# Modulation vectors as columns that are spread under a matrix of ones, eleven spectrum buffers, and a new written-out order

## The chip, the cores and the metric

The kernel runs on one core of one Trainium2 chip. The metric is the device time of one execution in microseconds (us), lower is better; several executions are given as a median. A core has five engines with queues of their own: PE (TensorE: matmuls, with PEld for its weight loads), DVE (VectorE), ACT (ScalarE), POOL (GpSimd) and SP (SyncE, which here issues nearly all DMAs). Each engine takes its own instructions in the order in which they were written, and waits for others by semaphores. Matmul results land in PSUM; everything else lives in SBUF.

## The reference, cut to what matters

```python
x = A_q                                                  # 2048 x 640
sa, ca, ga, sb, cb, gb = split(silu(c) @ w_mod, 6)       # w_mod is 640 x 3840
h = layernorm(x) * (1 + ca) + sa
x = x + ga * A(h, k, v, ...)   # A: 4-tap conv of k, times v; a long convolution
                               # along the 2048 rows by FFT; y + kv * ssm_D; times h
h = layernorm(x) * (1 + cb) + sb
x = x + gb * B(h, ...)         # B: z = gelu(h @ w_in), halves z1 and z2;
                               # z2 = layernorm(z2); g = w_sp @ z2 + b_sp; (z1 * g) @ w_out
```

Everything is bfloat16 with 2048 rows, 640 channels and 1728 columns of `w_in` (two halves of 864).

## The kernel before, in words

**Layout.** `xt` holds the 2048 x 640 input as 16 row tiles of 128 partitions. `gh` holds, of the same shape, first the normalised x, then (by `gh_mod`, L648) that times `(1 + ca) * ga` plus `sa * ga`, so that the gate `ga` is already inside; for that, rows `gca1_bf` and `gsa_bf` (128 x 640, the same vector in every partition) are needed. `gb_bf` is the row of `gb`; it multiplies `w_o` in the last part. `cb` and `sb` are used as columns (channel on the partition).

**The loop over spectra.** Channels are taken in five units of 128 (`u` = 0 to 4). For every unit the filter (`XK`) and the signal (`XU`) go through a first transform stage (`s1`, copied by `s1c`), then eight steps `st` of a second one: `fwdK` on PE is copied by ACT into a `KH` tile (`khc`), `fwdU` on PE stays in PSUM (`pu`), DVE multiplies both (`prod`, L454), for six of eight steps two `csum` halves add up (L468, on POOL or DVE), `inv` on PE transforms back into `pz`, and `zc` (ACT or DVE) copies that into `Z`. For units 0 to 3 one DMA transpose (`zt`, L677) turns `Z` into `ZT`, of which there is one buffer; then PE does four `y` steps (`y u_0` to `y u_24`) and DVE multiplies them into `gh` (`ym`, L670). `res` (L690) adds `gh` into `xt`; `ln2` (L696) takes statistics. Unit 4 is turned on PE instead (`zfl`, copies `zk`, `yl`, `yml`).

**The signal.** k and v are loaded by DMA transposes (`ldk`, tag `big`, two buffers), convolved by PE (`taps`), multiplied by v on DVE (`tv`), written to a scratch in DRAM (`kvw`) and read back as `XU`.

**After the loop.** For each of four groups of four row tiles: `ag2`, `rstd2` (POOL), `nmr2`, `zx` (normalise, on DVE, ACT or POOL), turned on PE for group 0 (`hfl`, with `hmod` on DVE and ACT) and by a DMA (`turn`, with `hmod2`) for the others; then 16 `zz` matmul groups per row-tile group (5 matmuls of 432 columns each, alternating PSUM tags `pu` and `pz`, two buffers each), their gelus on ACT, and for the z2 half `stz`, `agz`, `rstdz`, `nmrz`, `zn`. Then comes the part that is not planned: `mix`, `project` (L969, L989).

**What sets the order.** `Plan.op` (L94) numbers every step as the code is built and records what it reads and writes. `Plan.run` (L112) then issues them in the order of the string `ORDER` (L40): each entry is an engine letter (P, A, D, G for POOL, S for SP) and a step's number. So `ORDER` fixes both the engine of a step and the order in each engine's queue. `FILLS` (L34) gives the lengths of dummy matmul groups (`fill`, L941) that write an `s1` PSUM tile. `SLOTS` (L36) gives the buffers per tag: KH=9, wm=1, T=3, sm=2, big=2, ZT=1.

**The modulation vectors.** `mod(j)` (L607) is called for j = 2, 1, 0, 3, 4, 5 (ga, ca, sa, sb, cb, gb). Each loads 640 x 640 weights `wm` (800 KB, one buffer). For j = 3 and 4 it makes columns: 25 matmuls with one moving column (`modc`), then a copy of 128x5. For the others it makes rows: per half of 320 columns five matmuls with `sc_rep` (silu(c) repeated 128 times, written by `scr` at L782) as weights (`modr`), so that every partition gets the row; then `gac` (ACT) for ga, `gcac` (DVE) for `(1 + ca) * ga`, `gsac` (DVE) for `sa * ga`, `gbc` (ACT) for gb. `gelut` (L784) is a one-element gelu that has the table for gelu loaded; nothing depends on it.

Of the kernel before, what the change touches and what calls it, by code (L numbers as in the profile page):

```python
# [10 lines left out]
ALU = mybir.AluOpType  # L11
# [4 lines left out]
P = 128  # L16
# [17 lines left out]
FILLS = (4, 6, 2, 2, 4, 3, )  # L34
MODE = ('susussus', 'susussus', 'susussus', 'susussus', 'susussus')
SLOTS = dict(Tf=2, W=2, X=3, X1=4, KH=9, T=3, Z=3, ZT=1, wm=1, big=2, dg=2, st1=2, s1=1, sm=2, pu=2, pz=2)  # L36
# [4 lines left out]
D0 D13 D100 G101 S88 A1 P1032 P7 A4 A10 G5 A23 D15 D102 D109 D103 D110 A112 D115 A111 S2 D6 P1033 P8 A11 D14 A16 D116  # L41
A117 A118 D104 A105 S19 P1034 P26 A106 D90 D121 S82 D86 D17 D122 D18 G119 G113 P1035 P145 A146 P148 D149 S21 S83 D87
P24 A124 A147 D27 D127 S20 A150 P227 A228 A114 P151 A123 A152 P154 A156 P28 D25 S22 A153 D29 D155 P233 A234 G125 A126
P30 S523 D31 D527 P139 D140 G120 S34 P161 A162 P163 S32 G107 P133 P229 G48 A164 S33 P169 A170 D134 D36 S3 P167 A168
A230 G108 P136 D137 P171 A172 P165 A166 P142 A143 G135 D528 P41 A128 D529 D530 D138 P157 A158 P159 A160 S35 G141 P231
A232 D42 S84 S85 P37 D38 P173 P176 A174 A175 D177 P43 D44 A178 P182 D183 P9 A12 G130 P179 A184 P39 D181 D40 A180 P185
D186 S524 A531 A532 P195 D196 P191 D192 S46 S47 P55 D56 A533 P247 A248 G187 G188 P189 S45 P211 D212 G197 G144 G198 P51
D52 A534 P201 D202 D535 P49 D50 G213 P205 G214 A190 S526 A542 P53 D206 P203 A204 G72 S89 P217 D218 G131 A543 P193 P221
D222 P251 A252 D194 P215 A216 A544 G536 D537 P235 P253 P199 D254 D54 A236 P241 A242 G60 S565 P566 G553 P257 A258 S525
D538 D539 S91 G207 G208 P237 P568 A238 P239 A240 P255 A256 G223 P245 D93 A246 P249 A250 S57 G549 G224 D554 G555 P225  # L50
A226 D200 P301 P259 D260 P291 D292 G556 P209 A302 P219 G261 G262 D540 S570 P303 A569 P269 A567 G550 G551 G552 D270
G271 P275 A304 A220 P573 D574 P307 A210 P571 D276 D572 G651 A308 P285 D286 D541 A545 P263 P293 S58 A294 P305 A306 P65
D614 P243 A264 P265 G707 D266 A244 D546 S92 P325 S59 D66 D672 G272 D593 A326 P63 D64 P315 A316 P327 D649 P273 G287
A328 P321 A322 D591 P267 A268 G288 P329 A330 S575 G547 D548 S70 P295 D296 D297 P578 D579 A274 P576 G561 D577 D562 D594
P313 A557 A314 P309 P331 A332 P61 D652 S94 D96 G298 D563 D564 G655 A310 P67 D62 P311 P375 D68 A312 P349 D350 P333 D334
P289 G597 D670 P73 A376 A558 A559 A560 P343 D344 P77 G598 P377 P317 A318 D129 A290 P277 A278 G335 D595 D596 A378 D653
G336 P323 A324 P299 D592 P337 A300 P319 A320 A338 G345 S71 D78 S599 G346 D74 D616 P379 A380 P369 G713 P600 G612 S69
P351 A352 P279 P347 D370 D601 P381 A382 P602 D280 D603 P365 P79 D366 D80 A348 G654 P604 P383 A384 S95 P399 A400 D605
P387 A388 P359 G281 G282 P283 A284 G371 G372 P401 A402 D360 P606 D607 G613 P353 D354 S97 P385 A386 D99 S580 D618 P403
A404 P75 P397 A398 P395 A396 D619 D671 P405 A406 P373 A374 P339 G361 G362 P363 A364 D615 P449 A450 G608 D76 P413 P367  # L60
A368 G355 D340 D414 P407 D408 P341 A342 G617 P453 G709 S620 P621 D622 G674 P393 D650 A454 P389 A394 A390 S81 G356 P623
D624 P451 A452 P439 D440 P357 A358 P625 D626 P391 A392 P455 P427 G409 G410 P627 P417 G609 P581 G673 G656 D428 G429
D430 A456 S98 P411 A412 D418 P471 A472 P473 D628 A474 D634 P431 P457 G419 G420 P443 P479 A458 D444 A480 D629 D632 P467
A468 P421 A432 P423 D424 G445 P475 A476 P433 D434 A582 S657 G639 A422 P415 G676 P461 A462 D631 P477 A478 D630 D638
P463 A464 P658 D659 A416 P465 A466 P441 A442 G446 P660 D635 P481 G435 P447 A448 P497 G710 D661 P662 G436 P437 A438
P425 A426 D482 D663 P664 D498 S583 P517 D518 G677 G483 G484 P485 A486 P507 D508 P499 P459 A460 P469 P501 A470 D665
G675 G519 G520 P521 A522 G509 G510 A500 A132 G708 P487 P584 D502 P513 D488 P511 A512 P491 P489 G503 A490 D514 P515
G504 D492 S678 G668 P505 P679 A516 A506 G493 D494 P495 A585 D633 D680 P681 D682 A496 P719 A720 D636 S586 P683 D684
P715 P721 A722 D716 P685 D686 D687 P717 A718 P587 A588 P723 P726 P725 G711 P724 G666 D688 D689 G714 D727 D728 D730
D729 D759 P735 P749 P589 A590 D758 D731 D732 G692 D690 G760 D761 D691 A762 G763 P1036 P1037 P764 D736 D733 P765 D771  # L70
D766 D767 D768 D734 D772 P742 G667 D693 D750 G773 D774 G775 D737 D740 D739 G610 D741 D738 D694 A769 S756 A770 P787
D637 P784 D696 A788 A776 S757 D695 D836 P818 G669 P791 A785 A792 P777 D835 D837 P778 D834 A782 A819 D779 D643 D780
D781 P816 A817 G838 D839 D840 D841 A783 P794 A795 P814 P820 A842 A821 D843 S844 G848 D697 D699 G845 A815 D702 D751
D753 D701 D712 D743 D700 D698 D744 D748 D903 P798 A799 P812 A813 P826 A827 D747 P805 A806 P808 P801 A809 P822 D703
D752 D642 D849 D754 A846 A847 D704 A802 P824 A825 P886 A823 D640 A887 P850 A851 D706 P853 D611 G644 A854 D641 P857
D745 A858 P884 D900 P874 D902 A885 D746 D901 G904 D905 A875 D906 D755 D909 D907 D800 P890 A891 P880 A881 P882 P892
G908 S910 A893 A883 D876 D705 P888 A889 G912 A911 P860 P871 D810 A872 D803 D646 D807 D967 P878 A861 A913 P864 D647
A865 P867 A879 A868 D915 D914 P958 D648 D969 P923 P916 A924 A917 P946 D786 A959 P944 D645 A947 D966 D968 G970 D971
D972 G973 D796 P937 D804 A938 D975 D789 D790 A945 P933 A934 P926 D793 D797 P930 A931 G974 S976 A981 D859 D869 D866
D870 A927 D811 G828 P954 A955 D918 P952 A953 P948 G978 D932 D935 D936 A979 P940 A941 P919 D939 A949 D829 A830 D873  # L80
D877 D942 D943 D928 G980 G977 P1020 A920 A1021 P982 A983 D925 D929 D921 A833 D852 D862 D863 P996 D855 D856 G894 D895
P1024 A1025 A997 D998 D922 P989 A990 D831 P992 D899 A993 P1006 A1007 P1003 D1008 P985 A1004 D991 A986 P1014 A1015 G960
D961 P956 A957 P999 P950 A1000 A832 D896 A951 P1010 A1011 D1005 D994 P1016 A1017 D898 D987 D984 D1001 D988 D1002 D995
P1022 D1009 G1026 D1027 A964 D1029 A1031 A965 P1012 D962 D1028 D897 P1018 A1019 A1023 A1013 D1030 D963
# [39 lines left out]
def kernel(  # L124
# [79 lines left out]
    with ExitStack() as actx:  # L204
        consta = actx.enter_context(tc.tile_pool(name="consta", bufs=1))
        gh = consta.tile([P, NT, D], BF16)
        ga = consta.tile([P, D], F32)
# [7 lines left out]
        sc_rep = consta.tile([P, ND, P], BF16)  # L215
# [53 lines left out]
        nc.gpsimd.memset(mhalf[:], -0.5)  # L269

# [336 lines left out]
        def mod(j):  # L607
# [6 lines left out]
            if j in (3, 4):  # L614
                ps = "mod%d" % j

                def cols(e):
                    p_ = new(ps, "sm", [P, 512], F32)
                    for i in range(ND):
                        for kt in range(ND):  # L620
                            mm(p_[:, i:i + 1], tl[wm][:, kt, i * P:(i + 1) * P], sc_bf[:, kt:kt + 1], kt == 0, kt == ND - 1)
                op("P", "modc", cols, r=[wm, "sc"], w=[ps], new=[(ps, "sm")])
                if j == 3:
                    op("A", "sbc", lambda e: e.copy(sb_col[:], tl[ps][:, 0:ND]), r=[ps], w=["sb"])
                else:
                    op("A", "cbc", lambda e: e.add(cb1_col[:], tl[ps][:, 0:ND], 1.0), r=[ps], w=["cb"])
                return
            for h in range(NH):
                ps, hs = "mod%d_%d" % (j, h), slice(h * HS, (h + 1) * HS)
                p_ = lambda ps=ps: tl[ps][:, 0:HS]  # L630

                def rows(e, ps=ps, hs=hs, p_=p_):
                    new(ps, "sm", [P, 512], F32)
                    for kt in range(ND):
                        mm(p_(), sc_rep[:, kt, :], tl[wm][:, kt, hs], kt == 0, kt == ND - 1)
                op("P", "modr", rows, r=[wm, "sc"], w=[ps], new=[(ps, "sm")])
                if j == 2:
                    op("A", "gac", lambda e, hs=hs, p_=p_: e.copy(ga[:, hs], p_()), r=[ps], w=[("ga", h)])
                elif j == 1:
                    op("D", "gcac", lambda e, hs=hs, p_=p_: e.scalar_tensor_tensor(  # L640
                        gca1_bf[:, hs], p_(), 1.0, ga[:, hs], op0=ALU.add, op1=ALU.mult), r=[ps, ("ga", h)], w=[("gca", h)])
                elif j == 0:
# [407 lines left out]
```

## Time and profile before

| what | us |
|---|---|
| median of four runs (318.89 to 321.42) | 319.88 |
| the profiled execution | 321.42 |
| its span | 319.6 |
| PE busy in the span | 307.7 |
| DVE busy | 205.5 |
| ACT busy | 153.2 |
| POOL busy | 113.2 |

The span is the time from the first to the last instruction of the profiled execution; 1.8 us lie around it. In the page's slices each digit is the busy share of a fortieth of the span in tenths. A line of the stretches gives start and end, length, then the busy time and number of instructions of PE, PEld, DVE, ACT and POOL, the clock granted to PE (1.00 is full), the share of the DMA engines' time and GB/s. A line of the order of time gives the start, the duration (of several alike, from the first start to the last end), the engine, the line of the code, the operation, output and inputs, shape, count, and in brackets how long the engine sat idle before it and what ended that. Matmuls overlap, so for PE the distance from one start to the next is what a step costs, not the duration shown.

### The profile page before, as it was taken

To read this page: it belongs to the slowest core of one execution; us is meant where nothing else is said; L and a number is where in the kernel's file an instruction comes from. 1 tells how busy PE (TensorE), PEld (TensorE's weight loads), DVE (VectorE), ACT (ScalarE), POOL (GpSimd) and SP (SyncE) were. 2 spreads that over 40 slices of the span, in tenths; PEclk is the share of its full clock that TensorE was granted. 3 is DMA by queue.
4 is the path that set the end of the run, shared out by engine and by line. 5 is a ranking of instruction groups with operands and counts; after the bars stand their busy time and mean duration, and the time that the engine had idled before them with its cause. 6 is when DMAs were issued, how large, how long until landed. Compare 5 with 4: busy or idle time off the path is not lost.

```text
span 319.6 us, 6393 instructions
## 1 busy us (share of the span) xinstructions
PE 307.7 (96%) x2570; PEld 204.3 (64%) x2577; DVE 205.5 (64%) x436; ACT 153.2 (48%) x273; POOL 113.2 (35%) x146
## 2 busy tenths in 40 slices
PE   7988899989999999999999999999999999999996
PEld 2755688758799988655555555555555555555554
DVE  7898998979999998898884872522222222333333
ACT  6987799978888867477667772000000000000001
POOL 2532877848987997544234310000000000000000
PEclk9999999999999999999999999999999999999999
DMA  8999999996988479022419960675556555522221
GB/s 167 205 229 227 239 297 246 216 188 161 237 201 159 128 144 368 4 42 41 84 33 161 184 174 2 131 165 106 134 115 117 115 115 117 115 51 49 49 51 62
DMA packets 127025, 45.00 MB, mean 141 GB/s; under 512 B 116143, under 2 KB 126228, under 8 KB 126996
## 3 DMA queue, kind: packets, MB, share of 16 engines
q1 hardware_dynamic: 126842, 44.55, 64.8%
q8 instruction: 20, 0.33, 0.4%
q14 instruction: 9, 0.07, 0.1%
q10 hardware_dynamic: 154, 0.05, 0.1%
HBM read 16.11 MB, written 5.24 MB: 67 GB/s over the span
## 4 chain that ended last, share of the span: by engine, by line
PE 60%; DMA 2%; DVE 1%; ACT 0%; issue 0%; SPq 0%
PE ps L974 29%; PE pz L237 10%; PE pu L237 10%; PE po L995 9%; DMA big<-in_B_w_in_dram 2%; PE sm L237 1%; DVE Tf L454 1%; PE s L237 1%; DVE T L454 0%; ACT X L240 0%; PE s L850 0%; DVE ot L997 0%; PE sm L850 0%; PE pt L986 0%; SPq L612 0%
## 5 line engine op out<-in xcount | busy, mean ns | idle before, releaser
L974 PE MATMUL ps<-X,wT 128*128 128x432 bf16 x512 | 95.7, 346 | 0.0
L974 PEld LDWEIGHTS <-wT 128*128 128x128 bf16 x512 | 50.1, 98 | 42.2
L987 ACT COPY uT<-pt 128x896 bf16<-128x896 bf16 x1 | 0.9, 906 | 118.5 <-PE pt L986 118.5
L237 PEld LDWEIGHTS <-Z 128*128 128x128 bf16 x320 | 31.1, 98 | 26.8 <-DVE Z L863 0.2
L237 PE MATMUL pu<-X,M 128*128 128x128 bf16 (+1 forms) x480 | 45.8, 237 | 2.5 <-DVE Tf L454 2.2
L237 PEld LDWEIGHTS <-M 128*128 128x128 bf16 x480 | 37.4, 98 | 8.9 <-issue 3.4
L977 DVE SCALAR_TENSOR_TENSOR u<-ps,bcol,G 128x432 bf16<-128x432 f32 x18 | 12.0, 667 | 42.3 <-PE ps L974 42.3
L468 POOL TENSOR_TENSOR W<-Tf 128x256 bf16<-128x256 f32 x47 | 34.8, 760 | 11.4 <-DVE Tf L454 7.9
L995 PE MATMUL po<-w_o,uT 128*128 128x320 bf16 (+2 forms) x231 | 33.2, 295 | 0.1
L240 ACT CAST X<-s 128x1024 bf16<-128x1024 f32 x31 | 31.8, 1027 | 2.7 <-PE s L237 2.4
L237 PE MATMUL pu<-big,Z 128*128 128x432 bf16 x160 | 32.6, 346 | 0.0
L237 PE MATMUL pz<-big,Z 128*128 128x432 bf16 x160 | 32.5, 346 | 0.0
L454 DVE TENSOR_TENSOR Tf<-pu,KH 128x1024 f32<-128x1024 f32 x25 | 30.3, 1219 | 2.8 <-POOL gh L600 1.1
L977 DVE SCALAR_TENSOR_TENSOR u<-ps,bcol,M 128x432 bf16<-128x432 f32 x14 | 9.3, 667 | 29.9 <-PE ps L974 29.9
L995 PEld LDWEIGHTS <-uT 128*128 128x128 bf16 (+1 forms) x231 | 22.2, 98 | 9.9 <-issue 0.2
L237 PEld LDWEIGHTS <-G 128*128 128x128 bf16 x330 | 24.7, 98 | 2.2 <-issue 0.4
L240 ACT CAST KH<-pu 128x512 bf16<-128x512 f32 x40 | 23.0, 600 | 5.2 <-PE pu L237 5.1
L240 ACT CAST Z<-pz 128x512 bf16<-128x512 f32 x38 | 22.3, 601 | 5.3 <-PE pz L237 5.1
L997 DVE TENSOR_TENSOR ot<-po,xt 128x320 bf16<-128x320 f32 (+1 forms) x33 | 15.9, 482 | 12.5 <-PE po L995 12.5
L237 PEld LDWEIGHTS <-X 128*128 128x128 bf16 x288 | 17.9, 97 | 7.1 <-DMA X<-kv_scr 2.4
L918 DVE BATCH_NORM_STATS2 stz<-X 128x6 f32<-128x432 bf16 x32 | 18.0, 589 | 4.8 <-ACT X L912 4.7
L237 PE MATMUL s<-F1bd,X 128*128 128x256 bf16 x128 | 19.2, 272 | 1.7 <-DVE X L392 1.3
(154 smaller groups left out, 423.6 us busy)
## 6 DMA issues: line engine op xcount, KB each, us to landing
wm<-in_w_mod_dram SPq DMA_DIRECT2D x6, 800.0 KB, 6.3
xt<-in_A_q_dram SPq DMA_DIRECT2D x4, 640.0 KB, 6.3
out_dram<-ot SPq DMA_DIRECT2D x15, 160.0 KB, 2.3
big<-in_B_w_in_dram SPq DMA_DIRECT2D x2, 1080.0 KB, 9.1
X<-in_A_ssm_k_dram SPq DMA_DIRECT2D x4, 512.0 KB, 5.5
kv_scr<-big SPq DMA_DIRECT2D x4, 512.0 KB, 4.0
X<-kv_scr SPq DMA_DIRECT2D x4, 512.0 KB, 4.8
w_o<-in_B_w_out_dram SPq DMA_DIRECT2D x6, 160.0 KB, 3.7
```

The lines of the kernel that those rows point to most:

```text
L237: nc.tensor.matmul(o, lhsT=w, rhs=x, start=start, stop=stop)
L240: (e.copy if e is nc.scalar else e.tensor_copy)(dst, src)
L454: e.tensor_tensor(T_[:], (tl[pu] if src is None else tl[src])[:, :, :, None, :].to_broadcast(shape), tl[KH][:, :, None, :, :].to_broadcast ...
L468: e.tensor_tensor(tl[W][:, :, o, :], T_[:, :, 0, o, :], T_[:, :, 1, 1 - o, :], op=ALU.add if o else ALU.subtract)
L918: op("D", "stz", lambda e, i=i, n=n, fc=fc: e.bn_stats(out=stz[:, n, fc, :], in_=tl[z2][:, i, fc * FC:(fc + 1) * FC]), r=[(z2, (i, fc))], ...
L974: nc.tensor.matmul(ps[:, :FC], lhsT=wTs[t][:, s_, :], rhs=tl["z2_%d" % (s_ // TB)][:, s_ % TB, fc * FC:(fc + 1) * FC], start=(s_ == 0), st ...
L977: nc.vector.scalar_tensor_tensor(u[:, sl], ps[:, :FC], bcol[:, t:t + 1], z1[t][:, sl], op0=ALU.add, op1=ALU.mult)
L987: nc.scalar.copy(uTs[t][:], pt[:])
L995: nc.tensor.matmul(ps[:, :hi - lo], lhsT=uTs[t][:fsz[ft], ft, :], rhs=w_o[:fsz[ft], ft, lo:hi], start=(ft == 0), stop=(ft == NFT - 1))
L997: nc.vector.tensor_tensor(ot[:, lo:hi], ps[:, :hi - lo], xt[:, t, lo:hi], op=ALU.add)
```

## The change

All six modulation vectors are made as columns (`modc`). Vectors 2, 1 and 0 are combined as columns on DVE (`mcs`: `(1 + ca) * ga` and `sa * ga`, 128x5 each), vectors 2 and 5 are copied (`mcc`). Where a row is needed (1, 0 and 5), the column is spread into a tile `md` of 128 x 640, the product of the identity and the column (`mdg`, DVE or POOL), and one matmul per half with a 128 x 128 matrix of ones as weights (`mbc`) adds up the partitions, so that every partition gets the row; a copy (`gbc`, DVE or ACT) takes it to SBUF. `sc_rep`, its writer `scr` and the float32 row `ga` go; `mcol` (128 x 4 x 5) and `ones` come. KH gets two more buffers. FILLS and ORDER are new.

```diff
-FILLS = (4, 6, 2, 2, 4, 3, )
+FILLS = (10, 4, 4, 4, 1, )
-SLOTS = dict(Tf=2, W=2, X=3, X1=4, KH=9, T=3, ...
+SLOTS = dict(Tf=2, W=2, X=3, X1=4, KH=11, T=3, ...
...
-        ga = consta.tile([P, D], F32)
+        mcol = consta.tile([P, 4, ND], F32)
+        ones = consta.tile([P, P], BF16)
-        sc_rep = consta.tile([P, ND, P], BF16)
+        nc.gpsimd.memset(ones[:], 1.0)
...
+            ps = "mod%d" % j
+            def cols(e):
+                p_ = new(ps, "sm", [P, 512], F32)
+                for i in range(ND):
+                    for kt in range(ND):
+                        mm(p_[:, i:i + 1], tl[wm][:, kt, i * P:(i + 1) * P], sc_bf[:, kt:kt + 1], kt == 0, kt == ND - 1)
+            op("P", "modc", cols, r=[wm, "sc"], w=[ps], new=[(ps, "sm")])
...
+            elif j == 1:
+                op("D", "mcs", lambda e: e.scalar_tensor_tensor(mcol[:, 1, :], src(), 1.0, mcol[:, 2, :], op0=ALU.add, op1=ALU.mult),
+                   r=[ps, ("mc", 2)], w=[("mc", 1)])
+            elif j == 0:
+                op("D", "mcs", lambda e: e.tensor_tensor(mcol[:, 0, :], src(), mcol[:, 2, :], op=ALU.mult), r=[ps, ("mc", 2)], w=[("mc", 0)])
+            else:
+                op("DA", "mcc", lambda e: copy(e, mcol[:, 2 if j == 2 else 3, :], src()), r=[ps], w=[("mc", 2 if j == 2 else 3)])
+            if j in (2, 3, 4):
                 return
+            row, key, c = {0: (gsa_bf, "gsa", 0), 1: (gca1_bf, "gca", 1), 5: (gb_bf, "gb", 3)}[j]
+            md = "md%d" % j
+            def spread(e):
+                new(md, "T", [P, ND, P])
+                e.tensor_tensor(tl[md][:], ident[:, None, :].to_broadcast([P, ND, P]),
+                                mcol[:, c, :, None].to_broadcast([P, ND, P]), op=ALU.mult)
+            op("DG", "mdg", spread, r=[("mc", c), "ident"], w=[md], new=[(md, "T")])
             for h in range(NH):
-                def rows(e, ps=ps, hs=hs, p_=p_):
-                    new(ps, "sm", [P, 512], F32)
-                    for kt in range(ND):
-                        mm(p_(), sc_rep[:, kt, :], tl[wm][:, kt, hs], kt == 0, kt == ND - 1)
+                def rows(e, ps2=ps2, hs=hs):
+                    p_ = new(ps2, "sm", [P, 512], F32)
+                    mm(p_[:, 0:HS], ones[:], tl[md][:].rearrange("p t q -> p (t q)")[:, hs], True, True)
+                op("P", "mbc", rows, r=[md], w=[ps2], new=[(ps2, "sm")])
+                op("DA", "gbc", lambda e, hs=hs, ps2=ps2: copy(e, row[:, hs], tl[ps2][:, 0:HS]), r=[ps2], w=[(key, h)])
```

The whole of ORDER is written anew, 1038 entries before and 1043 after. Where the prediction speaks of it, the two lists read as follows (names in place of numbers):

```
SP, from the load of filter unit 3 on
  before: XK3, kv4 v, zt 0, kvw 3, XU3, XK4, wm3, zt 1, kvw 4, XU4, zt 2, wm4, zt 3, wm5, w_in 1, w_in 0
  after:  XK3, kv4 v, zt 0, kvw 3, XU3, wm3, XK4, zt 1, kvw 4, XU4, zt 2, w_in 1, wm4, zt 3, wm5, w_in 0
SP, before it (the same in both): XK2, kvw 2, wm1, kv3 k, XU2, kv3 v, wm0, kv4 k
PE, last steps of unit 4 up to the first zz
  before: inv 4_4, y 3_0, inv 4_2, y 3_8, zfl 16, y 3_16, zfl 0, zfl 24, y 3_24, zfl 8, modr 5_0, yl 4_0 (four parts),
          yl 4_1, yl 4_3, modr 5_1, fill 4, fill 3, hfl (s1, sm), yl 4_2, zz z2 n0
  after:  y 3_0, inv 4_4, y 3_8, inv 4_2, y 3_16, zfl 0, zfl 8, y 3_24, zfl 24, (yl 4_0 first part), zfl 16, (three parts),
          modc 5, yl 4_1, yl 4_3, mbc 5_0, fill 4, fill 4, fill 1, hfl (s1, sm), yl 4_2, zz z1 n0
DVE, from the last product on
  before: prod 4_2, csum 4_2, ln2, ym 3_0, ym 3_8, ln2, ym 3_16, zk 0, ym 3_24, res, ln2, ln2, yml 4 g0
  after:  prod 4_2, csum 4_4, ym 3_0, csum 4_2, ln2, ym 3_8, ln2, ym 3_16, zk 0, ym 3_24, res, zk 16, ln2, ln2, yml 4 g0
POOL, around the first rstd2
  before: res 3 g1, rstd2 (first piece), zx 1        after: res 3 g1, mdg 5, rstd2 (first piece), zx 0
ACT
  before: gelut after zc 4_3, ahead of zc 4_5        after: gelut when two of the 64 gelus are left
  after, first zz: gelu, gelu, zx 3, gelu, gelu, hmod, gelu, hmod
SP loads of the first units: before XK1, Dr, kv0 k, XK0, kv0 v, XK0; after XK0, Dr, kv0 k, kv0 v, XK0, kv0 k, XK1
DVE, filter unit 3: addD 3 follows gsac and ghm before, mcs 0 after; the list after has mcs and mcc at 128x5 only
Engines, before to after: csum POOL 47 to 42 and DVE 3 to 8; ghm DVE 19 to 21; res DVE 11 to 15; xn DVE 4 to 1, POOL 8 to 11;
  zc DVE 2 to 4; zk DVE 1 to 2; zx DVE 8 to 4; hmod2 DVE 3 to 6; mdg POOL 3; gbc ACT 5 and DVE 1 (the last entry of DVE)
```

## The prediction

> **What bounds the kernel now.** First the page's busy shares and its slices, then the stretches, then the order of time at the places that the change touches.
>
> ```profile
> PE 307.7 (96%) x2570; PEld 204.3 (64%) x2577; DVE 205.5 (64%) x436; ACT 153.2 (48%) x273; POOL 113.2 (35%) x146
> PEclk9999999999999999999999999999999999999999
> ```
>
> PE is busy for 96% at full clock, so it looks like the only bound. The stretches, cut at the first spectrum product on DVE (28.9 us), the end of the last one (121.0), the first `zz` matmul (132.9) and the first `mix` matmul (191.9), say more:
>
> ```profile
> 28.90:121.00 92.10, 87.65 (x1076) 74.93 (x1079) 85.14 (x126) 77.87 (x135) 73.70 (x85) 1.00 0.95 205
> 121.00:132.90 11.90, 11.01 (x233) 9.18 (x231) 10.17 (x28) 6.87 (x12) 8.70 (x9) 1.00 0.60 214
> 132.90:191.90 59.00, 59.00 (x339) 31.85 (x336) 45.87 (x138) 42.55 (x79) 21.59 (x29) 1.00 0.53 98
> 191.90:319.60 127.70, 124.73 (x751) 72.57 (x749) 40.46 (x77) 3.14 (x5) 0.00 (x0) 1.00 0.43 94
> ```
>
> The columns after the length are PE, PEld, DVE, ACT, POOL. In the loop over spectra (92.1 us) PE, DVE, ACT and POOL are all 80 to 95% busy and feed each other in a ring; none is the bound alone. From 132.9 PE never stops: 64 `zz` groups of 0.913 us and 0.55 us of flips make 58.98 of the 59.0. The last 127.7 us are not touched. So the change can gain only before 132.9, and can lose there or in the `zz` stretch.
>
> **The change part by part**
>
> *PE work.* The order of time of PE has both ways to make a modulation vector:
>
> ```profile
> 43.47 0.84 PE L237 MATMUL sm<-wm,sc_rep 128*128 128x320 bf16 x5
> 44.14 0.27 PE L237 MATMUL s<-F1bd,X 128*128 128x256 bf16 x1
> ...
> 98.77 0.77 PE L237 MATMUL sm<-sc_bf,wm 128*128 128x1 bf16 x25
> 99.39 0.27 PE L237 MATMUL pz<-W,G 128*128 128x256 bf16 x1
> ```
>
> From start to the next start, a row half (`modr`) takes 0.68 us, a set of columns (`modc`) 0.62. A broadcast (`mbc`) is one matmul of 320 columns; a fifth of a `modr` is 0.135. Ahead of the first `zz`: 8 x 0.68 = 5.44 go; 4 x 0.62 and 5 x 0.135 = 3.16 come; the fills grow from 21 to 23 matmuls of 0.213 (0.43). PE has 1.85 us less. The sixth `mbc` (0.135) now stands inside the `zz` stretch.
>
> [...]
>
> *DVE, ACT, POOL.* Gone: `scr` (POOL 0.72), `gac` and `gbc` (ACT 0.50 and 0.43, two each), `gcac` and `gsac` (DVE 0.45 from start to start, two each). New: three spreads of 128x640 (`mdg`), all on POOL in the list; the nearest row is the diagonal of L530, 1042 ns for 128x512, so 1.30 us (as low as 0.85 at DVE's 682 ns row scaled alike); six copies of 128x320, five on ACT at 0.43; four of 128x5 at 0.12 to 0.2. The chain of a vector grows by spread and broadcast, about 2 us; the list has products and copies between its links, and for vectors 1 and 0 that is the cover. For vector 5 it is not (below).
>
> The list also moves work between engines. Counted from the first to the last product, DVE gets four `csum` halves (0.36), three `ghm*` (0.42), two `zc` (0.62) and three 128x5 copies (0.12) more, and two `ghm+` (0.40), four row products (0.45), three `xn` (0.50), one `ln2` (0.34) fewer: 1.44 + 1.26 + 1.24 + 0.36 - 0.80 - 1.80 - 1.50 - 0.34 = -0.14 us. DVE's load in the loop is unchanged. PE's there loses six `modr` (4.08) and gains three `modc` (1.86), four `mbc` (0.54), one `s1` (0.44) and one `y` (0.23): -1.0.
>
> *The start.* The first product waits for the scratch round trip of kv0, whose writes sit behind the same transposes on SP: no change in arrival (24.3). From there to the first forward transform PE has four `s1` and two `taps` in both lists (4 x 0.44 + 2 x 0.87) and a `gflip` (0.44) in place of a small turn (0.1): +0.35.
>
> *The loop.* With DVE equal and PE 1.0 lighter I take half, -0.5. One wait shows where more is to be had:
>
> ```profile
> 65.80 0.75 DVE L653 TENSOR_TENSOR gh<-gh,gsa_bf 128x512 bf16<-128x512 bf16 x2
> 68.74 0.23 DVE L392 TENSOR_TENSOR X<-X,D_col 128x16 bf16<-128x16 bf16 x1 [2.19 <-DMA X<-in_A_ssm_k_dram]
> ```
>
> DVE waits 2.19 us, and PE 1.29 behind it, for the fourth filter spectrum, which stands in SP's queue behind the load of modulation vector 1, and that behind the only weight buffer. One `modc` frees the buffer after 34.1 us of PE work, two `modr` after 35.3: the load can be 1.2 earlier. DVE gets to the wait with 34.3 us of work since the first product instead of 36.8, so it is there 2.1 earlier (after +0.35). The wait therefore does not shrink, its end comes up to 1.2 sooner, and 2.3 us of DVE work are owed behind it. Net: between -1.2 and +1.1; I take 0. The two further KH buffers (nine to eleven): PE's three waits on products (2.2 us) stand at forward steps of the signal, for PSUM, not for KH; bounded at 0 to -0.7 (DVE's one wait for a KH that is still to be written), taken as 0.
>
> *The single ZT buffer.* A turn of a spectrum can't be issued until PE has done the last `y` of the spectrum before; PE's work between must cover it:
>
> ```profile
> 98.55 4.85 SPq L677 DMA_TRANSPOSE ZT<-Z  x1
> 103.51 0.53 SPq L612 DMA_DIRECT2D wm<-in_w_mod_dram  x1
> ...
> 107.11 0.40 PE L237 MATMUL sm<-Ebd,ZT 128*128 128x64 bf16 x8
> ```
>
> Issue to use is 8.56 us here, and the median landing of these turns is 8.4. PE's list between `y` 1_24 and `y` 2_0 shrinks from 16 steps of 0.44 (forward, `s1`, summed `inv`), one of 0.885 (unsummed `inv`) and a `modc`, 8.54, to 17 and one, 8.36; between `y` 2_24 and `y` 3_0 from 12, three and a `modc`, 8.55, to 10, three and a `modc`, 7.67. With the 0.3 us that the release takes, the second is short by up to 1.0, less the waits that lie in it anyway (0.6): +0.4. PE takes its list in order, so `inv` 4_4 and 4_2 wait behind it.
>
> *From the last product to the first zz* (11.9 us). DVE has one `csum` half (now behind `ym` 3_0), three `ln2` and one `zk` more, one `ag2` fewer: 0.36 + 1.02 + 0.62 - 0.18 = +1.82; PE's `zfl` and `y` waits in it (0.4 + 0.3 + 0.4 of DVE idle) can take 1.1 of that: +0.7. POOL:
>
> ```profile
> 129.17 0.19 POOL L184 TENSOR_SCALAR rstd<-mv 128x2 f32<-128x2 f32 x1 [1.54 <-DVE mv L821]
> 129.44 0.80 POOL L185 TENSOR_TENSOR rstd<-rstd,mhalf 128x2 f32<-128x2 f32 x1
> ```
>
> It waits 1.54 us there; the spread of vector 5 now stands in that place, after a `modc` and a copy that follow the four `yl` 4_0: 127.5 + 0.62 + 0.3 + 1.30 = 129.7, so `rstd2` and all behind it (`zx`, `hfl`, `hmod`, first `zz`) come 0.5 later. `modr` 5_0 (0.68) leaves PE ahead of `yl` 4_0, but there PE waited for copies of ACT that take until 127.1, so nothing of it shows. The fills before `hfl` (7 now, 9 after) end about with the later `zx`: nothing more. I take +0.5 of POOL and, since both delays meet in the same chain, +0.3 of DVE's 0.7.
>
> *The zz stretch.* +0.135 (`mbc` 5_1). The table for gelu was loaded at 117.75, off the chain:
>
> ```profile
> 117.75 1.28 ACT L784 ACT_TABLE_LOAD   x1
> 119.04 0.20 ACT L784 ACTIVATE warm<-warm 128x1 f32<-128x1 f32 x1
> 119.15 0.57 ACT L240 CAST Z<-pz 128x512 bf16<-128x512 f32 x1
> ```
>
> In the new list `gelut` is ACT's third last entry, behind 62 gelus. The first gelu will bring its own load. If it runs while ACT waits for the second `zz` (1.8 us), it costs 0. If after, that gelu ends 1.82 + 0.2 + 1.28 + 0.5 = 3.8 us after the first `zz` begins, and the fifth `zz`, which needs its PSUM slot, would start at 3.65; `zx` 3, two gelus on, would come some 0.8 late for `hfl`. So 0 to 0.8; I take 0. [...] DVE does more of `res` and `ghm` here and reaches `zx` 12 at 31.9 us of its work instead of 27.6; ACT's `zx` 14 and 13 stand behind that before two gelus. The third turn then lands near 173.5 for a use near 178: covered.
>
> Sum: 0.35 - 0.5 + 0 + 0.4 + 0.8 + 0.15 = +1.2 us less what the ring absorbs; the waits at `y` 3_0 and the DVE load behind it are the same 0.4 counted at two ends, so +0.8. The profiled execution took 321.42 us, a span of 319.6 and 1.8 around it, and is the slowest of four; against the median, 319.88, I say 320.7.
>
> **The rivals**
>
> *Turns late (slower).* The first half of w_in (1080 KB, 9.1 us to landing) now leaves SP right behind the turn of spectrum 2, where 800 KB of wm4 left before, and wm4 follows. 3.5 us of the turn lie after its issue; doubled, `y` 2_0 waits +3.5 and everything behind it. For: 8.36 us of cover against 8.4. Against: wm4 already shared those 3.5 us without a wait. It decides from 1 us of extra landing time on. 319.9 + 0.8 + 3.3 = 324.0.
>
> *ACT is the bound of the first zz groups.* The load in line, `zx` 3 and `hfl` of the second piece late by all of it: +1.3. For: `gelut` is last. Against: ACT is idle before the first gelu. 322.0.
>
> *PE's saving comes whole (faster).* -1.85 in place of -0.5, the wait for spectrum 3 ends 1.2 sooner and DVE, with eleven KH, makes up the rest; the POOL delay goes under the fills. 0.35 - 1.85 - 1.2 - 0.7 + 0.135 = -3.3: 316.6. For: seven us of PE's loop are idle or wait. Against: DVE's load in the loop is the same to 0.14.
>
> **How the numbers follow.** Forecast 0.46 (own range 318.3 to 322.9), turns late 0.20, ACT 0.14, faster 0.20. A measurement of this kernel tells 1% (3.2 us) from no change: below 316.7, above 323.1. Faster by over 1%: half of the faster case and a little of the forecast, 0.13. Slower by over 1%: 0.16 of the turns, 0.03 of ACT, 0.05 of the forecast, 0.24. Within 1%: 0.63. The range runs from the faster case to a little over the turns: 316.4 to 324.8.
>
> **What would show it.** Right: `modc` at 0.62 and `mbc` at 0.13 to 0.14 from start to start; first `zz` about 0.7 us later than 132.9, `rstd2` right behind an `mdg`; a table load just ahead of the first gelu; 59.1 us from first `zz` to first `mix`; 127.7 after. Wrong: a wait of PE over 1 us at `y` 2_0 (turns), a gap of PE among the first ten `zz` (ACT), a first `zz` before 131 (faster), or a wait of the loop that none of these names.

## The result and the profile after

The kernel after takes 321.08 us in the median (43 runs, 318.12 to 324.06), the kernel before 320.02 (64 runs, 317.20 to 322.22). The ratio is 1.0031, 95% interval 1.0017 to 1.0044: 1.1 us slower, under 1%. Forecast were 320.7 and "within 1%". The total is right, but by luck: several of its terms are wrong, and they cancel. The ratio and its interval leave out the slowest runs, those over 1.5% above the fastest run of the same kernel.

The profiled execution is the fastest of the 43 (318.12 us, span 316.2). Its page has the same two lines as before:

```profile
PE 306.4 (97%) x2637; PEld 203.7 (64%) x2645; DVE 207.9 (66%) x449; ACT 150.1 (47%) x271; POOL 111.1 (35%) x143
PEclk9999999999999999999999999999999999999999
```

Its stretches, cut at the same events (first product on DVE, end of the last, first `zz`, first `mix`; columns as in the prediction):

```profile
29.00:116.50 87.50, 86.11 (x1124) 74.37 (x1129) 84.22 (x133) 76.25 (x133) 75.37 (x84) 1.00 0.96 223
116.50:129.40 12.90, 11.25 (x250) 9.16 (x249) 11.81 (x32) 5.73 (x10) 9.19 (x10) 1.00 0.29 106
129.40:188.50 59.10, 59.10 (x338) 31.91 (x335) 45.12 (x137) 43.84 (x80) 18.21 (x26) 1.00 0.37 70
188.50:316.20 127.70, 124.71 (x751) 72.55 (x749) 41.97 (x81) 3.24 (x6) 0.00 (x0) 1.00 0.49 106
```

Here the loop is 4.6 us shorter than in the profile before (92.1) and the way from the last product to the first `zz` 1.0 longer. One profile of the fastest execution doesn't explain a median that is slower. So both kernels were run again, and all profiles of this study are set side by side. "9th" is the ninth spectrum product on DVE, where the second spectrum begins; times in us:

| profile | first product at | first to 9th | 9th to end of last | last to first `zz` | `zz` to `mix` | span | mean granted clock |
|---|---|---|---|---|---|---|---|
| before | 28.9 | 20.2 | 71.9 | 11.9 | 59.0 | 319.6 | 1.000 |
| before_again | 28.3 | 20.6 | 70.5 | 11.9 | 59.0 | 318.0 | 1.000 |
| after | 29.0 | 18.3 | 69.2 | 12.9 | 59.1 | 316.2 | 1.000 |
| after_again | 29.6 | 21.4 | 69.4 | 14.0 | 59.1 | 321.1 | 0.995 |
| gelut_back | 30.2 | 19.7 | 69.5 | 12.9 | 59.1 | 319.2 | 1.000 |
| w_in_back | 30.0 | 19.5 | 68.6 | 14.9 | 59.1 | 319.8 | 0.993 |
| fills_early | 30.4 | 19.8 | 68.6 | 13.1 | 59.1 | 318.7 | 1.000 |
| mdg_late | 30.3 | 18.3 | 68.6 | 13.7 | 59.2 | 317.8 | 0.993 |
| kh9 | 29.5 | 23.2 | 68.6 | 12.9 | 59.1 | 321.5 | 0.995 |
| rows_back9 | 29.8 | 21.6 | 70.8 | 13.4 | 59.0 | 322.5 | 1.000 |
| v_first | 29.1 | 22.7 | 69.2 | 14.5 | 59.1 | 322.4 | 0.988 |
| v_tail | 29.4 | 19.7 | 69.2 | 12.3 | 59.3 | 317.7 | 1.000 |
| tail_warm | 31.0 | 19.5 | 68.7 | 12.3 | 59.3 | 318.6 | 1.000 |
| taps_tail | 29.2 | 20.0 | 68.6 | 12.3 | 59.5 | 317.3 | 1.000 |

Seven of these have the loop of the kernel after unchanged (after, after_again, gelut_back, w_in_back, fills_early, mdg_late, tail_warm). Against the mean of the two profiles of the kernel before, their means give +1.5 us at the start, -0.9 to the ninth product, -2.2 from there to the last; then, where the tail is unchanged too, +1.0 to the first `zz` where the clock was full (after, gelut_back) and +2.1 and +2.9 where it was not (after_again, w_in_back), and +0.13 in the `zz` stretch. Before rounding that is -0.6 us with a full clock and +0.5 and +1.4 without.

The small rows are as forecast: a `modc` 0.63 from start to start, an `mbc` 0.13 to 0.20, a table load ahead of the first gelu that costs nothing. In order of time, PE and ACT of the kernel after:

```profile
42.21 0.77 PE L238 MATMUL sm<-sc_bf,wm 128*128 128x1 bf16 x25
42.84 0.33 PE L238 MATMUL pu<-X,M 128*128 128x256 bf16 x2
...
58.27 0.56 PE L238 MATMUL sm<-T,ones 128*128 128x320 bf16 x2
58.67 0.60 PE L238 MATMUL pu<-X,M 128*128 128x256 bf16 x6
```

```profile
129.87 1.28 ACT L917 ACT_TABLE_LOAD   x1
131.41 0.53 ACT L917 ACTIVATE M<-pu 128x432 bf16<-128x432 f32 x1 [0.25 <-PE pu L238]
```

The first gelu waits 0.25 us for PE, not for the table, and PE has no gap among the first ten `zz`.

### The profile page after: what moved, and what is told of

The parts are those of the page before. It is cut to its first block, busy times and chain, and to the rows that moved or that the text cites. A ratio compares the mean times of both kernels' runs of the same rounds, so it can differ in the third digit from the quotient of the medians.

```text
span 316.2 us, 6540 instructions
## 1 busy us (share of the span) xinstructions
PE 306.4 (97%) x2637; PEld 203.7 (64%) x2645; DVE 207.9 (66%) x449; ACT 150.1 (47%) x271; POOL 111.1 (35%) x143
## 4 chain that ended last, share of the span: by engine, by line
PE 84%; SPq 5%; DVE 4%; DMA 2%; issue 2%; ACT 2%; POOL 1%; DVEq 0%
PE ps L979 30%; PE pu L238 18%; PE pz L238 16%; PE po L1000 10%; PE sm L238 5%; PE s L238 4%; SPq L515 3%; DVE Tf L456 2%; DMA big<-in_A_v_dram 2%; POOL W L470 1%; DVE T L456 1%; ACT X L241 1%; SPq L753 1%; ACT KH L241 1%; SPq L384 1%
## 5 line engine op out<-in xcount | busy, mean ns | idle before, releaser
L470 POOL TENSOR_TENSOR W<-Tf 128x256 bf16<-128x256 f32 x42 | 31.9, 774 | 4.7 <-DVE Tf L456 3.8
L241 ACT CAST X<-s 128x1024 bf16<-128x1024 f32 x30 | 30.9, 1029 | 2.4 <-PE s L238 2.2
L456 DVE TENSOR_TENSOR Tf<-pu,KH 128x1024 f32<-128x1024 f32 x25 | 30.4, 1215 | 1.5 <-PE pu L238 1.0
L241 ACT CAST Z<-pz 128x512 bf16<-128x512 f32 x36 | 21.1, 602 | 5.8 <-PE pz L238 5.8
L238 PE MATMUL sm<-big,dg 128*128 128x512 bf16 (+3 forms) x72 | 19.1, 379 | 0.6
```

Of the source, the lines that this page charges most:

```text
L238: nc.tensor.matmul(o, lhsT=w, rhs=x, start=start, stop=stop)
L241: (e.copy if e is nc.scalar else e.tensor_copy)(dst, src)
L456: e.tensor_tensor(T_[:], (tl[pu] if src is None else tl[src])[:, :, :, None, :].to_broadcast(shape), tl[KH][:, :, None, :, :].to_broadcast ...
L470: e.tensor_tensor(tl[W][:, :, o, :], T_[:, :, 0, o, :], T_[:, :, 1, 1 - o, :], op=ALU.add if o else ALU.subtract)
```

## The experiments

Two theories were set against each other from the repeated runs on. *Clock*: the new way to the first `zz` lets the granted TensorE clock fall in most executions. *Draw*: only the loop's length varies, and the rest is chance. Later ones are named where they come up. Each ratio below is against runs of the kernel before that were taken beside it; their median lay between 319.1 and 320.8 us, so ratios are to be compared, and not times of different experiments.

**after_again and before_again: both kernels as they are, on one chip.**

> The changed kernel, unchanged, looked at once more. Its first profiled execution took 318.1 us, the least of 43; the median is 321.1. Theory 'draw': the loop over spectra varies from execution to execution with the landing of DMAs, and the 87.9 us of that one were luck; then this profile shows a loop of 90 to 92 us with waits of PE that the first did not have, and 320 to 322 us in all, at full clock. Theory 'clock': the loop is 88 us every time, and the typical execution loses 1.5 to 3 us because PE is granted less than full clock somewhere; then the slices show a PEclk under 9 in one place and the stretches before it are as short as in the first.

> The kernel before, once more, as a second draw and as a measure of what two runs of one kernel differ by. Ratio 1.000 within 0.3%. Theory 'draw': the loop is again 90 to 93 us here, or moves by 2 us and more against the first. Theory 'clock': the loop is 92.1 within 0.5 and the clock 1.00.

Measured: after_again 321.26 us, ratio 1.0007 (0.9973 to 1.0041); before_again 320.51, 0.9989 (0.9959 to 1.0019). The profile of after_again fell on an execution with mean granted clock 0.995. Its windows (PE, PEld, DVE, ACT, POOL, then the granted clock):

```profile
126.00:128.00 2.00, 1.60 (x64) 1.60 (x65) 1.93 (x6) 0.51 (x2) 0.96 (x2) 1.00 0.00 0
128.00:130.00 2.00, 2.00 (x51) 1.57 (x48) 1.90 (x9) 0.37 (x1) 1.83 (x3) 0.54 0.03 8
130.00:132.00 2.00, 1.94 (x7) 0.59 (x5) 1.84 (x6) 0.98 (x2) 1.70 (x3) 0.61 0.00 0
132.00:134.00 2.00, 1.89 (x34) 1.24 (x32) 0.45 (x2) 0.24 (x1) 0.49 (x1) 1.00 0.00 0
```

The clock is at half for 3.4 us, from 128.2 to 131.6 in windows of 0.5 us, and just there stand the nine fill matmuls that `hfl` has to queue behind. In order of time on PE, first after, then after_again:

```profile
125.43 2.54 PE L238 MATMUL s<-ident 128*128 128x512 bf16 x9
128.03 0.49 PE L855 MATMUL s<-ident,Z 128*128 128x128 bf16 x6
```

```profile
129.39 3.51 PE L238 MATMUL s<-ident 128*128 128x512 bf16 x9
132.95 0.49 PE L855 MATMUL s<-ident,Z 128*128 128x128 bf16 x6
```

The fills take 3.51 instead of 2.54 us, and DVE, ACT and POOL are nearly idle until `hfl` (last window: 0.45, 0.24, 0.49 busy of 2.00). From the end of the last product to `hfl` it is 12.63 us instead of 11.57 (132.95 - 120.32, 128.03 - 116.46): the stretch costs 1.06 us in this execution. A mean clock of 0.995 is one such stretch (3.4 x 0.5 / 320). Counted over all runs whose clock is listed: below 0.997 in 38 of 54 executions of the kernel after and in 3 of 114 of the kernel before. The list gives the mean alone and not the place. The medians: after 321.33 us below 0.997 and 320.16 above; before 320.01 above. So at full clock the kernels are about level, and executions below 0.997 are 1.2 us longer. This compares executions that chance has sorted; fills_early, mdg_late and tail_warm below act on the tail itself. *Draw* is seen as well: from the first product to the last it is 87.5 us in after and 90.8 in after_again.

**gelut_back: the gelu table loaded in the loop again, ahead of `zc` 4_5.**

```diff
-ACT: ... gbc 5_0, ..., (62 gelus), gelut, ...
+ACT: ... gelut, zc 4_5, ...
```

> The changed kernel with the warm-up gelu put back where it stood, ahead of zc 4_5. In the changed kernel's profile the table load ran in ACT's wait for the second zz (1.28 us from 129.87, gelu at 131.41 after 0.25 us of idle). Forecast's theory (hidden): no change, 321.1 within 0.5, and the load now on ACT at about 113, where it delays two zc by up to 1.3 us: up to +0.5. Rival (ACT bounds the first zz groups): 0.8 to 1.3 us faster, 320.

Measured: 321.3 us, ratio 1.0018 (0.9988 to 1.0048), not to be told from after_again. No effect of the place of the table load is seen, as forecast.

**w_in_back: the first half of w_in behind wm5, where the kernel before has it.**

```diff
-SP: zt 2, w_in 1, wm4, zt 3, wm5, w_in 0
+SP: zt 2, wm4, zt 3, wm5, w_in 1, w_in 0
```

> The changed kernel with the load of the first half of w_in put back behind wm5, as it was. Rival 'turns late': the turn of spectrum 2 was delayed in typical executions; then this is 1 to 3.5 us faster, 318 to 320. Forecast's theory: turns have their cover; within 0.5 of 321.1.

Measured: 322.72 us, ratio 1.0063 (1.0027 to 1.0099), 11 of 12 executions below 0.997 of the clock, four of them at 0.989 or less (in the profile of v_first, at 0.988, matmuls are slowed at two places). Putting w_in back gains nothing, so *turns late* falls. Why the lower clock is seen even more often here stays open.

**fills_early: the fills in the pauses of PE.**

```diff
-FILLS = (10, 4, 4, 4, 1, )
+FILLS = (10, 4, 2, 3, 4, )
-PE: mbc 5_0, fill, fill, fill, hfl
+PE: fill x2, zfl 4_0 ... yl 4_0 b3, fill x3, yl 4_0 b2 ... mbc 5_0, fill x4, hfl
```

> The kernel after with its nine late fill matmuls laid out differently: two ahead of the first `zfl` piece, three ahead of the third `yl` piece of group 0, four (instead of nine) ahead of `hfl`; same number in all. Theory `clock` (the tail's stream of 16-column and 1-column matmuls lets the granted TensorE clock fall to 0.5 for a stretch of about 3.4 us just where the fills and hfl run, which costs 1.0 to 1.5 us in the executions that it hits): the pauses of 0.45 and 0.51 us are filled, mean granted clock 1.0 in most executions instead of in 16 of 54, median about 320.2, 0.9 below the kernel after. Theory `tail` (the tail is 1 us longer by its own work, clock or not): hfl up to 0.5 us earlier since only four fills stand ahead of it, clock as before, median about 320.7. Theory `draw` (the loop's length varies and the tail is no matter): 321.1.

Measured: 320.09 us, ratio 1.0027 (1.0004 to 1.0049), 4 of 12 executions below 0.997. The low clock becomes rarer, as *clock* says, but the ratio gains little on 1.0031: the three fills stand behind the pause, not in it, so `yl` b2 and the chain behind it are 0.65 us late, and in its profile `hfl` waits 1.09 us for `zx`. The four executions with the low clock are no longer than the eight others here (medians 319.7 and 320.7), which speaks against a fixed price of the low clock; no profile shows where it fell in them.

**mdg_late: the spread of vector 5 off POOL's way.**

```diff
-POOL: mdg 5, rstd2 0 0, zx 0          PE: mbc 5_0, fill x9, hfl
+POOL: rstd2 0 0, zx 0, mdg 5          PE: fill x7, hfl ... mbc 5_0, mbc 5_1 (in the zz stretch)
```

> The kernel after with `mdg` 5 on POOL behind rstd2 and zx 0 instead of ahead of them, `mbc` 5_0 and its copy moved into the zz stretch beside 5_1, and seven late fills instead of nine. Theory `tail`: rstd2 starts 0.7 us earlier, hfl about 0.9 us earlier (the norm's end 0.5 and two fills 0.43, of which the later counts), zz 0.14 longer, median about 320.3. Theory `clock`: the half-clock stretch still falls on fills and hfl in over half of the executions, so the median moves by 0.4 at most, about 320.7. Theory `draw`: 321.1.

Measured: 320.49 us, ratio 1.0052 (1.0017 to 1.0087), 10 of 12 executions below 0.997. POOL reaches `rstd2` sooner (8.55 us behind the last product instead of 8.88), but in its profile the fills are still slowed (seven take 3.51 us, 1.89 in before; the page's PEclk digit is 8 from 127.1 to 135.1 us), which eats it. Neither part alone brings the ratio down, so later versions take both.

**kh9 and rows_back9: buffers and columns taken apart.** kh9 is the kernel after with nine KH buffers. rows_back9 is kh9 with the vectors of the kernel before in the new list (KH 9, because `sc_rep` and `ga` leave no room for more).

```diff
-SLOTS = dict(..., KH=11, ...)
+SLOTS = dict(..., KH=9, ...)
```

```diff
-modc j, mcc/mcs j, mdg j, mbc j_0, gbc j_0, mbc j_1, gbc j_1
+modr j_0, modr j_1, gac/gcac/gsac/gbc j_0, j_1
```

> The kernel after with nine KH buffers instead of eleven, list unchanged. Theory `buffers` (the two buffers are what took the 2.19 us wait for XK3 and the KH waits off the loop): the loop 1.5 to 3 us longer, about 323. Theory `list` (the order with its earlier transposes and loads did it): within 0.4 of the kernel after, about 321.2.

> The kernel after with the kernel before's modulation vectors (each of vectors 2, 1, 0 and 5 as two products of five 320-column matmuls against the replicated sc, no columns, no spreading), in the new list at the places of the new steps, and nine KH buffers, as the wider tiles leave no room for more. Against kh9. Theory `columns` (the PE work saved in the loop is time saved): 1 to 2 us slower than kh9 in the loop. Theory `list`: same loop as kh9. Theory `clock`: with ten 320-column matmuls of vector 5 in the tail instead of 25 of one column the half-clock stretch is seen in under a third of the executions, and the median is 0.7 below what the loop alone would give.

Measured: kh9 321.25 us, ratio 1.0050 (1.0020 to 1.0080); rows_back9 323.12, 1.0106 (1.0078 to 1.0133). From the ninth product to the last, first kh9, then rows_back9:

```profile
52.66:121.27 68.61, 67.99 (x918) 59.74 (x921) 66.26 (x101) 58.35 (x98) 60.60 (x67) 1.00 0.92 207
```

```profile
51.39:122.19 70.80, 69.69 (x898) 60.89 (x901) 67.56 (x102) 57.72 (x95) 56.20 (x63) 1.00 0.87 198
```

PE is busy for 99% of kh9's stretch and 98% of rows_back9's. The columns take 1.70 us off PE and 1.30 off DVE there, and the stretch is 2.19 shorter: with PE that full, its saving comes whole in this part. Over all, the medians differ by 1.87 us, which suggests that without the columns the new list would lose (it was written for them). Two KH buffers fewer leave the stretch at 68.61, among the shortest: `buffers` falls for this part, and the intervals of kh9 and after overlap. kh9's one long piece lies earlier (23.2 us to the ninth product). A wait of the same kind is in after_again (DVE 2.34 us, 3.1 in kh9), and in kh9 the eight `taps` matmuls at its end take 3.30 us instead of 1.89, with the page's PEclk digit at 8 from 40.2 to 48.2 us, so the length can't be laid to the buffers. rows_back9 is below 0.997 in 1 execution of 6, kh9 in 7 of 12. That fits a clock that holds with ten 320-column matmuls of vector 5 in the tail instead of 25 of one column; six executions do not show it, and in kh9's profile the clock is 1.00 in the tail (126 to 132 us) and the page's only digit below 9 lies in the loop.

**v_first: the wait ahead of the ninth product.** In the fast profile of after DVE goes straight on at the products of v block 2; in after_again it waits for that block's load:

```profile
35.10 1.28 DVE L547 TENSOR_TENSOR big<-sm,big 128x512 bf16<-128x512 f32 x2
```

```profile
38.97 1.29 DVE L547 TENSOR_TENSOR big<-sm,big 128x512 bf16<-128x512 f32 x2 [2.34 <-DMA big<-in_A_v_dram]
```

```diff
-SP: ldx 3, kvw 1, kv2 v, XU1
+SP: ldx 3, kv2 v, kvw 1, XU1
```

> The kernel after with one step of SP's queue moved: the transposing load of v for block 2 (`ldkv kv2 v`) ahead of `kvw 1`, as the kernel before has it, instead of behind it, where it stands behind SP's wait for the products of block 1. Theory `late v` (the new list lets DVE's `tv 2_2` wait for that load by 0 to 3.1 us, 0 in the fastest execution and 1.2 to 3.1 in five of six others with the same loop, and all engines with it): the load is issued near 26.5 instead of 29, the wait `DVE big <- DMA big` at 35 to 39 is gone, products 4 to 8 take 13.3 us instead of up to 15.6, and the median is 1.0 to 1.5 below the kernel after, 0.997 of the kernel before. Theory `traffic` (the load is slow because of what else moves then, not because of its place): the wait stays, time as after; and kvw 1 later by the load's 3 us could make the first products on XU1 wait, at most +1.

Measured: 322.53 us (six runs), ratio 1.0091 (1.0057 to 1.0126), above that of after. DVE no longer waits for v, but `kvw` 1 leaves later and PE waits for the spectrum that reads it back:

```profile
38.13 0.60 PE L241 MATMUL pu<-X,M 128*128 128x256 bf16 x6
41.19 0.99 PE L241 MATMUL s<-F1bd,X 128*128 128x256 bf16 x4 [2.45 <-DMA X<-kv_scr]
```

At the end of this wait the four `s1` and 12 `inv` matmuls take 0.99 and 1.91 us (0.60 and 1.24 at the same place in after), and in the tail the nine fills take 4.12 us instead of 2.54, at a mean clock of 0.988: the 22.7 us to the ninth product are not the wait alone. `late v` falls in this form. `traffic` has its second half right: the wait goes over to the next transfer.

**v_tail and tail_warm: both cures of the tail.** v_tail has v_first's queue, tail_warm that of the kernel after.

```diff
-FILLS = (10, 4, 4, 4, 1, )
+FILLS = (10, 4, 2, 2, 2, 3, )
-POOL: mdg 5, rstd2 0 0, zx 0
+POOL: rstd2 0 0, zx 0, mdg 5
-PE: zfl 4_0 ... yl 4_0 b3 ... yl 4_3, mbc 5_0, fill x9, hfl
+PE: fill x2, zfl 4_0 ... fill x2, yl 4_0 b3 ... fill x2, yl 4_3, fill x3, hfl ... mbc 5_0, mbc 5_1
```

> v_first, and the tail laid out anew: `mdg` 5 behind rstd2 and zx 0 on POOL, `mbc` 5_0 and its copy in the zz stretch, and the nine fill matmuls as two ahead of the first `zfl`, two ahead of the fourth `yl` piece of group 0 (where PE waits 0.45 and 0.51 us), two ahead of `yl 4_3` and three ahead of hfl. Theory `tail`: last product to first zz 11.8 us instead of 12.9 at full clock, against v_first 1.0 less in the median. Theory `clock`: half-clock stretches in fewer than half of the executions instead of three quarters, which takes another 0.5 off. If both hold and the late v too, 0.992 of the kernel before. If neither holds: as v_first.

> The kernel after with the tail of v_tail alone (`mdg` 5 behind rstd2 and zx 0, `mbc` 5_0 in the zz stretch, the nine fill matmuls as 2, 2, 2 and 3 in the pauses) and SP's queue as in after. Theories `tail` and `clock` together: last product to first zz 12.3 us where no half-clock stretch falls on it, such stretches in under half of the executions, median 1.0 to 1.5 below the kernel after, that is 0.998 to 1.000 of the kernel before. Theory `draw`: as after, 1.003.

Measured: v_tail 320.97 us, ratio 1.0047 (1.0015 to 1.0078), 1.56 below v_first; tail_warm 319.94, ratio 0.9975 (0.9948 to 1.0001). Below 0.997 of the clock are 5 of 12 and 4 of 12 executions instead of 38 of 54. PE of tail_warm in order of time:

```profile
124.64 0.59 PE L241 MATMUL s<-ident 128*128 128x512 bf16 x2
125.30 0.56 PE L241 MATMUL sm<-Ebd,X 128*128 128x16 bf16 x16
...
128.37 0.81 PE L241 MATMUL s<-ident 128*128 128x512 bf16 x3
130.14 0.51 PE L858 MATMUL s<-ident,Z 128*128 128x128 bf16 x6 [0.97 <-POOL Z L845]
```

Two fills now stand where PE had paused 0.51 us, and `hfl` waits for its data instead of for fills. POOL, first after, then tail_warm:

```profile
123.99 1.26 POOL L643 TENSOR_TENSOR T<-ident,mcol 128x640 bf16<-128x640 bf16 x1 [1.04 <-ACT mcol L241]
125.34 0.19 POOL L185 TENSOR_SCALAR rstd<-mv 128x2 f32<-128x2 f32 x1
```

```profile
127.76 0.19 POOL L188 TENSOR_SCALAR rstd<-mv 128x2 f32<-128x2 f32 x1 [2.05 <-DVE mv L829]
...
130.05 1.26 POOL L646 TENSOR_TENSOR T<-ident,mcol 128x640 bf16<-128x640 bf16 x1
```

From the end of the last product, `rstd2` starts after 8.17 us in before, 8.88 in after and 8.54 in tail_warm (127.76 - 119.22): 0.34 of the delay is the spread, 0.37 DVE's (mdg_late, which moves the spread and leaves the fills in their block, has 8.55). From there to `hfl` it is 2.41, 2.69 and 2.38: 0.28 are the fills. PE of before at that place:

```profile
129.63 1.89 PE L237 MATMUL s<-ident 128*128 128x512 bf16 x7
131.58 0.49 PE L850 MATMUL s<-ident,Z 128*128 128x128 bf16 x6
```

Through the kernel before, tail_warm stands at 0.994 of the kernel after (0.9975 / 1.0031), or at 0.997 by after_again (0.9975 / 1.0007), whose interval overlaps its own. So a gain on the kernel after is likely, and its size is open between 0.3 and 0.6%. tail_warm is the only changed version with a ratio under 1; its interval just reaches past 1.

**taps_tail: tail_warm with the products of v block 2 moved back.**

```diff
-DVE: prod 0_5, tv 2_2, tv 2_1, prod 0_4, tv 2_0, tv 2_3, prod 0_6
+DVE: prod 0_5, prod 0_4, prod 0_6, tv 2_2, tv 2_1, zc 0_2, tv 2_0, tv 2_3
(PE: the two taps for tv 2_0 and 2_3 some steps later)
```

> tail_warm, and in the loop the products that wait for the load of v for block 2 moved back: DVE's `tv 2_2` and `2_1` behind the products 0_4 and 0_6, `tv 2_0` and `2_3` and PE's taps for them some four steps later; SP's queue as in after. Theory `late v` in its second form (the load cannot come sooner, but what stands behind it need not wait): products 4 to 8 take 13.3 to 13.8 us in place of 13.3 to 17.8, median 0.8 to 1.2 below tail_warm. Theory `traffic` (every transfer of this stretch is late together, so the next one, the load of XU1, ends the same wait): as tail_warm, a wait for `X <- kv_scr` in place of that for v.

Measured: 320.53 us, ratio 1.0000 (0.9971 to 1.0028). The wait for v is gone, but DVE waits for PE ahead of the products instead, and from the fifth product to the ninth it takes 15.0 us (13.3 to 15.6 in the seven profiles with the loop of after):

```profile
36.34 1.23 DVE L459 TENSOR_TENSOR Tf<-pu,KH 128x1024 f32<-128x1024 f32 x1 [0.92 <-PE pu L241]
...
39.02 1.28 DVE L550 TENSOR_TENSOR big<-sm,big 128x512 bf16<-128x512 f32 x2
```

So neither form of `late v` brought the gain that it forecast. What sets the length up to the ninth product (18.3 to 23.2 us in the new list) and the start (29.0 to 31.0) was not settled; the same load of v block 2 occupies SP's queue for 3.0 us in the profile of after (from 28.88) and for 5.5 in after_again (from 29.69).

## Why the prediction was right in sum and wrong in parts

- **PE's work** (0.62, 0.13, the fills): right, by the rows above. The 25 matmuls of a `modc` follow one another in 0.63 us, with 25 weight loads beside them (PEld from 42.10 to 42.88 in after).
- **"With DVE equal and PE 1.0 lighter I take half, -0.5."** Wrong, and so is "none is the bound alone". Behind the ninth product PE is 97% busy already in before (69.76 of 71.88 us), and there the stretch shrinks by 2.2 us in the mean, in kh9 against rows_back9 by 2.19. The share of 95% was the average of two parts: a start with PE at 88% (17.89 of 20.22 us), which in after_again waits 2.26 us behind the load of v, and a rest that PE bounds. The rest in before, before_again and after:

```profile
49.12:121.00 71.88, 69.76 (x893) 60.59 (x895) 66.50 (x99) 59.43 (x94) 57.66 (x65) 1.00 0.93 187
48.93:119.38 70.45, 69.42 (x893) 60.61 (x895) 66.50 (x99) 59.22 (x94) 57.63 (x65) 1.00 0.91 190
47.28:116.46 69.18, 68.46 (x918) 59.69 (x921) 66.94 (x101) 58.59 (x98) 60.66 (x67) 1.00 0.94 208
```

  PE's work in it falls by 1.0 to 1.3 us, as forecast, and comes whole; the remainder is idle time of PE, 2.1 and 1.0 us in the two profiles of before and 0.7 in after.
- **XK3: "The wait therefore does not shrink", net 0.** Wrong. DVE's wait is 0.30 us in after and 0.66 in after_again, against 2.19 in before and 0.97 in before_again; it is part of the 2.2. Counted from the ninth product, the load leaves SP after 11.9 and 12.0 us instead of 13.4 and 13.4, and DVE is at the wait 1.0 to 1.2 us sooner; the forecast, counting from the first product, had 1.2 and 2.1. And 1.2 of the 2.19 were one execution's: from issue to use the load took 6.2 us there and 4.7 to 5.0 in the three other profiles.

```profile
63.82 1.12 DVE L394 TENSOR_TENSOR X<-X,D_col 128x16 bf16<-128x16 bf16 x1 [0.30 <-DMA X<-in_A_ssm_k_dram]
```

- **KH: 0.** Right behind the ninth product; ahead of it not settled.
- **ZT, +0.4.** Wrong: PE has no wait at `y` 3_0 in the profile of after (116.40, 8.4 us after the issue).
- **The start, +0.35.** Mis-sized: +1.5 in the mean, between +0.4 and +2.4, cause open.
- **Last product to first `zz`, +0.8.** The chain is +0.71 to `rstd2` (0.34 POOL, 0.37 DVE; forecast 0.5 and 0.3). **"The fills before `hfl` (7 now, 9 after) end about with the later `zx`: nothing more"** is the step that failed: they add 0.28 us at full clock, and in after_again `hfl` starts 1.56 us after the last `zx` (131.39 to 132.95), at half clock, which no step had considered: the sum took the clock to be full, as in the one profile of before.
- **The `zz` stretch, +0.15, table load 0.** Right (+0.13).
- **Rivals.** Turns late and ACT: not seen. *PE's saving comes whole* holds from the ninth product on; the later start, the longer tail and the half clock give it back. Its sign, a first `zz` before 131, was seen in the profile of after (129.4) although the median is slower: that sign belonged to the fastest execution.

Sum as measured, before rounding: 1.45 - 0.93 - 2.23 + 0.99 + 0.13 = -0.6, and about 1.2 for a clock below 0.997 in 38 of 54 executions (0.8): +0.2 from profiles, +1.1 from the medians. The rest stays open; the length up to the ninth product alone varies by 3 us between the seven profiles of one loop. The forecast of +0.8 met the +1.1 because a gain in the loop that it took too small stands against a start and a half clock that it missed: that is luck.

## What to carry to other kernels

Split a loop's busy shares where its supply changes before calling nothing the bound: one part may wait for transfers while PE bounds the other, and there a saving on PE was worth its full size here (1.70 us off PE, 2.19 off the stretch). When a change brings single-column matmuls and pauses into a stretch, look at the list of granted clocks of all runs, not at one profile. Here fillers did better in the pauses ahead of a critical step than in a block in front of it (4 of 12 executions below 0.997 in fills_early and in tail_warm, 38 of 54 in after). A wait on a transfer that goes away under one order may only move to the next transfer (2.34 us for v in after_again, 2.45 for `kv_scr` in v_first), so measure the stretch and not the wait.

## What the runs showed of the hardware that was not expected

The granted clock falls to 0.50 for 3.4 us and returns to 1.00, though PE is not idle before it: in after_again it was busy for 1.60 of the 2 us from 126.0, with 16-column and 1-column matmuls and a pause of 0.51 us just ahead of them, and the fall comes at 128.2. In w_in_back windows of 0.5 us show 0.50 for 3.4 us as well, from 127.7 to 131.1. In mdg_late, kh9 and v_first the mean clock (0.993, 0.995, 0.988) and matmuls that take longer show a lower clock; its length there is not shown. One stretch of 3.4 us at 0.50 gives a mean of 0.995 by estimate; where the rest of the 0.993 of w_in_back lies is not shown either. Whether the small matmuls or the pauses do it, no run here separates: tail_warm has the same small matmuls with pauses filled and is below 0.997 in 4 of 12 executions. Nor does a run show what sets the length, or why the same program is below 0.997 in some executions (38 of 54) and not in others. The tail of kh9 was busy for 1.49 of 2 us at about the same place (126 to 128) and kept the full clock.

In kh9 and v_first matmuls are slowed in the loop, at the end of a wait of PE of 3.03 and 2.45 us. The eight `taps` matmuls behind it in kh9 take 3.30 us, against 1.89 in after and also in after_again, where PE waited 2.26 us before them:

```profile
39.98 3.30 PE L238 MATMUL sm<-big,dg 128*128 128x512 bf16 x8 [3.03 <-DVE big L547]
```

```profile
35.85 1.89 PE L238 MATMUL sm<-big,dg 128*128 128x512 bf16 x8
```
